# Half-batch 4 of a fused attention and gated feed-forward kernel: k and q transposed by DMA through a DRAM scratch instead of on TensorE

## The chip, the cores and the metric

The kernel runs on one core of a Trainium2 chip. The metric is the device time of one execution in microseconds (us), as the median of several executions. A profile of one execution, with the start and length of every instruction, is used to explain it. TensorE (PE in the profile, PEld for its weight loads) multiplies matrices, VectorE (DVE), ScalarE (ACT) and GpSimd (POOL) work on tiles, SyncE (SP) issues DMAs, and GpSimd issues DMAs too.

## The reference

For 8 batches, 8 heads, 576 positions and a head dimension of 64, the reference does causal attention with a decay, and then a gated feed-forward block on the 4,608 tokens:

```
scores = q @ k.T / sqrt(D)
bias   = -(cumsum(max(s, 0))[i] - cumsum(max(s, 0))[j])
scores = where(causal, -1e9, scores + min(bias, 0))
attn   = exp(scores - max); attn = attn / (sum(attn) + 1e-9)
x      = attn @ v                     # tokens by 512
out    = (silu(x @ w_gate) * (x @ w_val)) @ w_out
```

The inputs are float32, w_gate and w_val are 512 x 1536, w_out is 1536 x 512, the output is 4,608 x 512 float32.

## The kernel before

**Work and its units.** The 64 pairs of batch and head are numbered 0 to 63; I call each a head. Four heads are a half-batch, so there are sixteen, 0 to 15, two to a batch. A head's scores are made in four pieces (`score_piece`, L338), each a few matmuls of k by q into one PSUM bank (L359) and an exponential on ScalarE (L369). GpSimd clears the masked part of the first and the last piece (L374, L379). The product with v (`av_piece`, L396) goes into another bank, and `av_out` divides: a reciprocal (L412) and a multiply (L413) on VectorE, which free that bank. A head pair's result is transposed into XT, for batches 0 and 1 on TensorE (`x_pe`, L446, with a copy at L453), later by DMA (`x_out`, `x_in`).

**Feed-forward.** Nine blocks of 512 tokens (`ffn_items`). In each, twelve pairs of gate and value products (L630), with tanh on ScalarE (L651) and two VectorE operations (L653, L664), then the products with w_out (L687 in blocks 0 and 1, L736 later). Block 0 works on the first 512 tokens while the heads from 8 on are attended to.

**How k and q get their shape.** The score matmuls read the tiles KQ, with the head dimension on the partitions. There are two sets of KQ tiles, for even and odd half-batches; each set has two tiles, one for the first two heads and one for the last two. The loads bring k and q with positions on the partitions (`load_qk`, L140), so each half-batch is cast to bf16 (`cast_one`: L246 on GpSimd for half-batches 2 to 5, L244 on ScalarE from 6 on) and transposed, in one of two ways:

- On TensorE, for half-batches 0 to 4 (0 in halves, L301): `pe_transpose` (L287) writes five or four 128x128 transposes into a PSUM bank, and `pe_out` copies the upper and the lower half out, on ScalarE (L314) or VectorE (L316). For half-batch 4 the list `PREP_AT[3]` puts the four groups behind chosen score pieces of half-batch 3.
- By DMA, for half-batches 5 to 15: `scratch` (L260) stores the cast tiles to DRAM (ks and qs), `transposes` (L270) brings them back transposed into pk and pq, and `split` (L274) copies the two halves into KQ on VectorE. The splits stand in the list `later` and are taken from it by `do_later`.

Four further rows of each KQ tile come by small DMAs (`aug`, L183).

**What sets the order.** The order is written by hand: each engine takes its instructions in the order in which the Python code issues them. `attn_items` (L548) is a generator over the heads; `pump` runs it to a position that follows from how far the feed-forward block has come (L1016 to L1034). `side` issues, after given score pieces, the loads, scratch stores, DMA transposes and splits; `side_v` (L518) casts v. In the code h is the half-batch whose scores are being made and step the head within it. An engine's or a queue's instruction that waits holds back everything that stands behind it on the same engine.

**Around the change.** While half-batch 3 is attended to (heads 12 to 15), the SP queue holds the loads of k and q of half-batches 4 and 5, the five loads of V 2 (v of batch 2, `load_v`, after the last piece of head 12), the loads of half-batch 6, and then the scratch stores and transposes of half-batch 5. There is one buffer for loaded v (rawv), so V 2 waits for the casts of V 1. GpSimd casts V 2 (L168) while half-batch 4 is attended to. Eight PSUM banks are shared: `take` gives the one that has been free longest, and in the second part of block 0 four of them are held by the products with w_out.

Of the kernel before, what the change touches and what calls it, by code (L numbers as in the profile page):

```python
# [19 lines left out]
def kernel(  # L20
# [14 lines left out]
    B, H, S, D = q.shape  # L35
# [6 lines left out]
    NHB = BH // HB  # L42
    NR = HB // 2
# [33 lines left out]
        tc.tile_pool(name="dram", bufs=1, space=bass.MemoryType.DRAM)  # L77
    )

    NPE = 5  # L80
    XB = 2
    KS = {i: dram.tile([NR * S, 128], BF16, name=f"ks{i}") for i in range(NPE, NHB)}
    XS = {
        i: dram.tile([NCH * 128, 128], BF16, name=f"xs{i}") for i in range(XB * H // 2, BH // 2)
    }
    QS = {i: dram.tile([NR * S, 128], BF16, name=f"qs{i}") for i in range(NPE, NHB)}

# [16 lines left out]
    first = first_sbuf.enter_context(tc.tile_pool(name="first", bufs=1))  # L104
# [5 lines left out]
    with tc.manual_schedule():  # L110
# [36 lines left out]
        def load_qk(hb):  # L147
            load_one(hb, "k")
            load_one(hb, "q")

        def load_v(b, cs, eng=nc.sync):
            if 0 in cs:
                loaded["v", b] = raw.tile([128, NCH, H, D], FP32, tag="rawv", bufs=1, name="rawv")
            t = loaded["v", b]
            for c in cs:
                n = 128 if c < 4 else TAIL
                eng.dma_start(
                    t[0:n, c, :, :],
                    v[b, :, c * 128 : c * 128 + n, :].rearrange("h p d -> p h d"),
                )  # L160

        def cast_v(b, c, eng):
            n = 128 if c < 4 else TAIL
            dst, src_t = VT[b % 2][0:n, c, :, 0:D], loaded["v", b][0:n, c, :, :]
            if eng is nc.scalar:
                nc.scalar.copy(dst, src_t)
            else:
                eng.tensor_copy(dst, src_t)  # L168
# [89 lines left out]
        def scratch(hb):  # L258
            for name, SC in (("k", KS), ("q", QS)):
                nc.sync.dma_start(  # L260
                    SC[hb].rearrange("(x j) c -> x (j c)", j=J),
                    cts[name, hb].rearrange("x j r d -> x (j r d)"),
                )
# [3 lines left out]
        def transposes(hb):  # L267
            for name, SC in (("k", KS), ("q", QS)):
                prs[name, hb] = cp.tile([128, NR * S], BF16, tag="p" + name, bufs=1, name="p" + name)
                nc.sync.dma_start_transpose(prs[name, hb], SC[hb])  # L270
# [185 lines left out]
        later = []  # L456

        def do_later(n):
            while n > 0 and later:
                f, *args = later.pop(0)  # L460
                f(*args)
                n -= 1
# [5 lines left out]
        def side(h, step, ci):  # L468
            bh = HB * h + step
            for c in V1_AT.get((bh, ci), ()):  # L470
                cast_v(1, c, nc.gpsimd)
            if bh == H + 4 and ci == 3:
                load_v(2, range(5))
            if h == 4 and (step, ci) in ((0, 1), (2, 1)):
                load_qk(6 + step // 2)
            if h >= 5 and h + 3 < NHB and (step, ci) == (0, 1):
                load_qk(h + 3)
            hb = h + 1
            if NPE <= hb < NHB:
                late = hb == NPE  # L480
                if late and (step, ci) == (0, 1):
                    scratch(hb)
                if late and (step, ci) == (0, 3):
                    transposes(hb)
                if (step, ci) == (0, 1):
                    aug(hb, GP4)
                first = 1 if hb < NPE + 3 else 0
                if step in (first, first + 1) and ci == (3 if late else 1):
                    for r in range(NR):
                        later.append((split, hb, "kq"[step - first], r))  # L490
            hb = h + 2
            if hb == NPE and step == 3 and ci % 2 == 1:
                cast_one(hb, "kq"[ci // 2], nc.gpsimd)
            if NPE < hb < NHB:
                six = hb == NPE + 1
                if (step, ci) == ((2, 0) if six else (0, 2)):
                    cast_one(hb, "k", nc.scalar)
                if (step, ci) == ((2, 2) if six else (1, 2)):
                    cast_one(hb, "q", nc.scalar)
                if (step, ci) == ((3, 0) if six else (2, 0)):  # L500
                    scratch(hb)
                if (step, ci) == (3, 3 if six else 0):
                    do_later(NR * 2)
                    transposes(hb)
            if ci != 1:
                return
            bn = h // 2 + 1
            if 3 <= bn < B:
                if h % 2 == 0:
                    if step == 2:  # L510
                        load_v(bn, (0, 1))
                    if step == 3:
                        load_v(bn, (2, 3, 4))
# [13 lines left out]
        def prep_one(hb, i, eng=None):  # L527
# [7 lines left out]

        PREP_AT = {
            2: {(1, 2): 0, (2, 0): 2, (2, 2): 1, (3, 0): 3},
            3: {(1, 3): 0, (2, 1): 1, (2, 3): 2, (3, 1): 3},
        }

        AV_AT = {
# [6 lines left out]
        def attn_items():  # L548
            for kk in range(H, BH + 2):
                h, step = divmod(kk, HB)  # L550
                if kk < BH:
                    if step == 0:
                        do_later(NR * 2)
                    if step == 1 and 3 < h + 1 < NPE:
                        cast_one(h + 1, "k", nc.gpsimd)
                        cast_one(h + 1, "q", nc.gpsimd)
                    if step == 2 and 3 < h + 1 < NPE:
                        aug(h + 1, GP4)
                    for ci in range(4):
                        score_piece(kk, ci)  # L560
                        side(h, step, ci)
                        side_v(h, step, ci)
                        yield kk + 0.1 + ci / 8
                        if (step, ci) in PREP_AT.get(h, ()):
                            prep_one(
                                h + 1, PREP_AT[h][step, ci],
                                (nc.scalar, nc.vector)[ci // 2] if h == 2 else None,
                            )
                            yield kk + 0.1 + ci / 8
                for x in X_AT.get(kk, (kk - 2,)):  # L570
                    if x % 2 == 1 and H <= x < BH:
                        if x < XB * H:
                            x_pe(x // 2)
                            yield kk + 0.5
                        else:
                            x_in(x // 2)
                for p in AV_AT.get(kk, (kk - 1,)):
                    if H <= p < BH:
                        av_piece(p, (0, 1, 2))
                        yield kk + 0.6  # L580
                        av_piece(p, (3,))
                        yield kk + 0.7
                        av_piece(p, (4,))
                        av_out(p)
                        if p >= XB * H and p % 2 == 1:
                            x_out(p // 2)
                        yield kk + 0.8
# [416 lines left out]
        for tt in range(NTT):  # L1004
            lo = H * (tt + 1) + LAGS[tt]
            hi = min(H * (tt + 2) + LAGS[tt + 1], BH + 2)
            span = 36 if tt < FIRST7 else 34.5
            if hi == BH + 2:
                span = 30
            n0 = 5 if tt == 0 else 0  # L1010
            n = 0
            todo = {FIRST7 - 1: W_SUMS, FIRST7: W_DIFFS}.get(tt, [])
            if tt == FIRST7:
                for _ in range(3):
                    weight_op(*todo.pop(0))
            for i, cost in enumerate(ffn_items(tt)):  # L1016
                n += cost
                if todo and (i >= 24 if tt < FIRST7 else i % 2 == 1):
                    weight_op(*todo.pop(0))
                if tt == 0 and n > 30:  # L1020
                    pass
                elif i >= 2 * NFT or i % (2 if tt == 1 else 4) == 1:
                    do_later(1)
                if seconds:
                    seconds.pop(0)()
                for f in hook.pop(n, ()):
                    f()
                done = min(1.0, max(0, n - n0) / (span - n0))
                if tt == 0:
                    done = (  # L1030
                        0.57 * max(0, n - n0) / (24 - n0) if n < 24
                        else min(1.0, 0.57 + 0.43 * (n - 24) / (span - 24))
                    )
                pump(lo + (hi - lo) * done)  # L1034
# [31 lines left out]
```

## Time and profile before

| what | value |
|---|---|
| median of 3 runs | 376.51 us (376.23, 376.51, 377.41) |
| span of the profiled execution, first to last instruction | 375.9 us |
| median less span: what lies around the span | 0.6 us |
| TensorE busy | 364.4 us, 97% of the span, at a granted clock of 1.00 throughout |
| VectorE, ScalarE, GpSimd busy | 290.4, 240.3 and 212.1 us |
| DMA queue of SP, queue of GpSimd | 41.46 and 22.21 MB, 45.9% and 22.6% of the 16 DMA engines' time |
| HBM | 37.90 MB read, 19.86 MB written |

The profile gives the span of its one execution and no time of its own for what lies around it, so a sum is made against the span, and the rest is taken from the median. A span of 375.9 us in 40 slices makes a slice of 9.4 us; a digit of 9 in the rows by slice means busy for nine tenths of it or more. The chain is followed back from the last instruction; a piece of it names the engine, what it writes, and the line. Lines of the views are those of the kernel before.

### The profile page before, as it was taken

To read this page: it belongs to the slowest core of one execution; us is meant where nothing else is said; L and a number is where in the kernel's file an instruction comes from. 1 tells how busy PE (TensorE), PEld (TensorE's weight loads), DVE (VectorE), ACT (ScalarE), POOL (GpSimd) and SP (SyncE) were. 2 spreads that over 40 slices of the span, in tenths; PEclk is the share of its full clock that TensorE was granted. 3 is DMA by queue.
4 is the path that set the end of the run, shared out by engine and by line. 5 is a ranking of instruction groups with operands and counts; after the bars stand their busy time and mean duration, and the time that the engine had idled before them with its cause. 6 is when DMAs were issued, how large, how long until landed. Compare 5 with 4: busy or idle time off the path is not lost.

```text
span 375.9 us, 8800 instructions
## 1 busy us (share of the span) xinstructions
PE 364.4 (97%) x3300; PEld 231.1 (61%) x3300; DVE 290.4 (77%) x578; ACT 240.3 (64%) x471; POOL 212.1 (56%) x325
## 2 busy tenths in 40 slices
PE   7699999999999999999999999999999999999995
PEld 6475556655555556855685558655865585476464
DVE  8867867458995899679976997599858867975984
ACT  8687777597986887578757876687465523323321
POOL 8982556665365657494649555955675416315320
PEclk9999999999999999999999999999999999999999
DMA  7899999799599998796869665995132103002003
GB/s 237 197 267 265 201 248 272 216 312 242 169 185 267 246 255 221 168 275 217 224 145 262 192 162 163 264 188 145 39 104 77 35 19 127 2 0 90 24 0 113
DMA packets 97146, 64.23 MB, mean 171 GB/s; under 512 B 77232, under 2 KB 82736, under 8 KB 97104
## 3 DMA queue, kind: packets, MB, share of 16 engines
q1 hardware_dynamic: 84976, 41.46, 45.9%
q0 software_dynamic: 12128, 22.21, 22.6%
q8 instruction: 26, 0.43, 0.5%
q14 instruction: 16, 0.13, 0.1%
HBM read 37.90 MB, written 19.86 MB: 154 GB/s over the span
## 4 chain that ended last, share of the span: by engine, by line
PE 90%; POOL 3%; ACT 2%; DVE 2%; DMA 1%; issue 1%; DVEq 0%; POOLq 0%; ACTq 0%
PE bank L630 47%; PE bank L736 17%; PE bank L359 11%; PE bank L396 8%; PE bank L687 6%; ACT pt L369 2%; DMA kq<-HL 1%; DVE kq L316 1%; PE bank L446 1%; DVE pp L653 1%; PE bank L287 1%; POOL vt L168 1%; DVE ht L664 1%; PE bank L353 1%; ACT kq L314 0%
## 5 line engine op out<-in xcount | busy, mean ns | idle before, releaser
L369 ACT ACTIVATE pt<-bank 128x512 bf16<-128x512 f32 (+1 forms) x256 | 120.3, 510 | 32.1 <-PE bank L359 18.9
L630 PE MATMUL bank<-XT,wg 128*128 128x512 bf16 x432 | 111.4, 379 | 0.5 <-DVE pp L653 0.3
L630 PE MATMUL bank<-XT,wv 128*128 128x512 bf16 x432 | 110.9, 379 | 0.1
L651 ACT ACTIVATE th<-bank 128x512 bf16<-128x512 f32 x108 | 64.7, 599 | 55.7 <-PE bank L630 51.1
L653 DVE SCALAR_TENSOR_TENSOR pp<-th,bank 128x512 bf16<-128x512 bf16 x108 | 73.7, 682 | 18.7 <-ACT th L651 18.2
L664 DVE SCALAR_TENSOR_TENSOR ht<-pp,bank 128x512 bf16<-128x512 bf16 x108 | 74.1, 687 | 10.6 <-PE bank L630 0.4
L359 PE MATMUL bank<-kq 128*128 128x128 bf16 (+4 forms) x576 | 75.8, 240 | 2.7 <-DMA kq<-HL 2.3
L673 POOL TENSOR_TENSOR ht<-ht 128x512 bf16<-128x512 bf16 x35 | 40.4, 1155 | 52.3 <-DVE su L671 52.2
L359 PEld LDWEIGHTS <-kq 128*128 128x128 bf16 x576 | 45.8, 98 | 33.1 <-DMA kq<-HL 2.6
L630 PEld LDWEIGHTS <-wv 128*128 128x128 bf16 x432 | 38.4, 98 | 36.4 <-issue 0.6
L630 PEld LDWEIGHTS <-wg 128*128 128x128 bf16 x432 | 38.3, 98 | 34.2 <-issue 0.7
L374 POOL TENSOR_SCALAR_AFFINE_SELECT pt<-pt 128x512 bf16<-128x512 bf16 x56 | 37.0, 661 | 30.8 <-ACT pt L369 23.4
L396 PEld LDWEIGHTS <-pt 128*128 128x128 bf16 x960 | 41.7, 98 | 17.3
L396 PE MATMUL bank<-vt,pt 128*128 128x65 bf16 x960 | 46.9, 194 | 0.3 <-POOL vt L168 0.3
L430 POOL DMA_DIRECT2D xs<-ot x24 | 21.7, 904 | 30.0 <-DVE ot L413 27.7
L736 PEld LDWEIGHTS <-ht 128*128 128x128 bf16 x336 | 31.2, 98 | 4.3
L413 DVE TENSOR_TENSOR ot<-bank,rc 128x320 bf16<-128x320 f32 x64 | 31.5, 492 | 2.2
L183 POOL DMA_DIRECT2D kq<-HL x48 | 28.7, 599 | 0.0
L687 PE MATMUL bank<-wo,ht 128*128 128x512 bf16 x96 | 25.8, 379 | 0.0
L736 PEld LDWEIGHTS <-su 128*128 128x128 bf16 x252 | 23.6, 98 | 3.3
L412 DVE RECIPROCAL rc<-bank 128x5 f32<-128x5 f32 x64 | 12.1, 189 | 15.3 <-PE bank L396 14.8
L801 POOL TENSOR_TENSOR ysb<-ysb 128x512 f32<-128x512 f32 x12 | 15.2, 1271 | 15.3 <-DVE ysb L795 15.3
(93 smaller groups left out, 389.1 us busy)
## 6 DMA issues: line engine op xcount, KB each, us to landing
out_dram<-ysb POOLq DMA_DIRECT2D x32, 256.0 KB, 3.9
rawv<-in_v_dram SPq DMA_DIRECT2D x28, 256.0 KB
rawk<-in_k_dram SPq DMA_DIRECT2D x12, 576.0 KB
rawq<-in_q_dram SPq DMA_DIRECT2D x12, 576.0 KB
xs<-ot POOLq DMA_DIRECT2D x24, 160.0 KB, 4.0
ks<-ck SPq DMA_DIRECT2D x11, 288.0 KB
qs<-cq SPq DMA_DIRECT2D x11, 288.0 KB
rawk<-in_k_dram POOLq DMA_DIRECT2D x3, 576.0 KB, 6.8
```

The source lines that it names most:

```text
L359: nc.tensor.matmul(sc[:, o : o + w], T[:, 1, e * S + 128 * tj : e * S + 128 * (tj + 1)], T[:, 0, e * S + lo : e * S + hi], start=not maske ...
L369: nc.scalar.activation(pt[:, c0 : c0 + n], sc, AF.Exp, scale=0.125)
L374: nc.gpsimd.affine_select(pt[:, 1088:1600], pt[:, 1088:1600], pattern=[[0, 4], [1, 128]], compare_op=ALU.is_ge, fill=zreg, base=0, channel ...
L396: nc.tensor.matmul(av[:, bi * (D + 1) : (bi + 1) * (D + 1)], pt[:, c0 : c0 + 128], VT[b % 2][:, tj, h, :], start=(tj == 0), stop=(tj == bi),)
L413: nc.vector.tensor_mul(ot[:, :, e * D : (e + 1) * D], av3[:, :, 0:D], rc[:, :, None].to_broadcast([128, NCH, D]),)
L630: nc.tensor.matmul(view(bs, TT), w[:, c, f0 : f0 + 128], xt[:, c, :], start=(c == 0), stop=(c == 3),)
L651: nc.scalar.activation(th, pg, AF.Tanh, scale=0.5)
L653: nc.vector.scalar_tensor_tensor(pp, in0=th, scalar=1.0, in1=pg, op0=ALU.add, op1=ALU.mult)
L664: nc.vector.scalar_tensor_tensor(hp[:, 2 * k2 : 2 * k2 + 2, :].rearrange("p a n -> p (a n)"), in0=pp, scalar=0.5, in1=pv, op0=ALU.mult, op ...
L673: (nc.vector if ft == NFT - 1 else nc.gpsimd).tensor_sub(hp[:, 1:3, :], hp[:, 1:4:2, :], hp[:, 0:3:2, :])
L687: nc.tensor.matmul(view(pys[ts_], DM), hps[ft // 2][:, 2 * (ft % 2) + half, c0 : c0 + 128], WO[j][:, ft % WKO, :], start=(ft == 0), stop=( ...
L736: nc.tensor.matmul(ps, lhs(p), rhs(p), start=(first and p == 0), stop=(last and p == NP - 1), skip_group_check=True,)
```

## The change

Half-batch 4 goes over to the DMA path. The 18 transposes on TensorE and the eight copies out of PSUM go; two scratch stores and two DMA transposes are added on SP's queue, and four splits on VectorE. The scratch stores are issued after the last score piece of head 13, the transposes after the first score piece of head 14. The loads of V 2, so far issued after the last piece of head 12, now stand behind these transposes on the same queue. The four splits go into `later` after the last pieces of heads 14 and 15; the loop of block 0 now takes them from there one at a time, and the rest is taken before head 16. The casts, the small DMAs of `aug` and the treatment of half-batches 5 to 15 stay: where NPE (5) stood for the first half-batch of the DMA path, NSC (5) now stands for the first that is treated by the general rule.

```diff
-    NPE = 5
+    NPE = 4
+    NSC = 5
...
-            if bh == H + 4 and ci == 3:
-                load_v(2, range(5))
+            if h == 3:
+                if (step, ci) == (1, 3):
+                    scratch(4)
+                if (step, ci) == (2, 0):
+                    transposes(4)
+                    load_v(2, range(5))
+                if (step, ci) in ((2, 3), (3, 1)):
+                    for r in range(NR):
+                        later.append((split, 4, "kq"[step - 2], r))
...
-            if NPE <= hb < NHB:
-                late = hb == NPE
+            if NSC <= hb < NHB:
+                late = hb == NSC
...
         PREP_AT = {
             2: {(1, 2): 0, (2, 0): 2, (2, 2): 1, (3, 0): 3},
-            3: {(1, 3): 0, (2, 1): 1, (2, 3): 2, (3, 1): 3},
         }
...
-                    if step == 1 and 3 < h + 1 < NPE:
+                    if step == 1 and h == 3:
                         cast_one(h + 1, "k", nc.gpsimd)
                         cast_one(h + 1, "q", nc.gpsimd)
-                    if step == 2 and 3 < h + 1 < NPE:
+                    if step == 2 and h == 3:
                         aug(h + 1, GP4)
...
                 if tt == 0 and n > 30:
-                    pass
+                    if later and later[0][1] == 4:
+                        do_later(1)
```

The DRAM tiles ks and qs of half-batch 4 are added by the first lines, since their range starts at NPE. In what is left out, NPE is replaced by NSC in the conditions for half-batches 5 and later, with the same value as before.

More of the change, by code (lines that the diff above doesn't have):

```diff
@@ L486, in side @@
                     aug(hb, GP4)
-                first = 1 if hb < NPE + 3 else 0
+                first = 1 if hb < NSC + 3 else 0
                 if step in (first, first + 1) and ci == (3 if late else 1):
@@ L491, in side @@
             hb = h + 2
-            if hb == NPE and step == 3 and ci % 2 == 1:
+            if hb == NSC and step == 3 and ci % 2 == 1:
                 cast_one(hb, "kq"[ci // 2], nc.gpsimd)
-            if NPE < hb < NHB:
-                six = hb == NPE + 1
+            if NSC < hb < NHB:
+                six = hb == NSC + 1
                 if (step, ci) == ((2, 0) if six else (0, 2)):
```

## The prediction

> **What bounds the kernel now.** I read the page first: busy shares, the slices, the chain by engine.
>
> ```profile
> span 375.9 us, 8800 instructions
> PE 364.4 (97%) x3300; PEld 231.1 (61%) x3300; DVE 290.4 (77%) x578; ACT 240.3 (64%) x471; POOL 212.1 (56%) x325
> DMA  7899999799599998796869665995132103002003
> PE 90%; POOL 3%; ACT 2%; DVE 2%; DMA 1%; issue 1%; DVEq 0%; POOLq 0%; ACTq 0%
> ```
>
> TensorE works 97% of the span and is 90% of the chain that ended last, so a TensorE instruction taken out anywhere is worth its own time, as long as nothing else becomes late. The DMA row says where that can fail: one slice is 9.4 us, and from the third to the fifteenth (19 to 141 us) the DMA engines are full but for a 7 in the eighth (66 to 75) and a 5 in the eleventh (94 to 103). The change takes time from the first resource and gives it to the second, at about 60 us.
>
> Next the chain around the four groups of transposes that go (start, length, what):
>
> ```profile
> 58.62 0.25 PE bank L359 x3
> 58.87 0.28 PE bank L287 x5
> 59.15 0.35 PE bank L446 x5
> ...
> 62.91 0.28 PE bank L287 x5
> 63.19 0.22 PE bank L359 x2
> ...
> 64.08 0.22 PE bank L287 x4
> 64.30 0.35 PE bank L446 x5
> ...
> 68.06 0.22 PE bank L287 x4
> 68.28 0.22 PE bank L359 x2
> ```
>
> From 54.98 to 87.23 us every piece of this chain is TensorE's, end to end, with no wait between. The L287 pieces are the transposes of half-batch 4: 18 in four pieces.
>
> Then SP's queue, for what is moved (start, length of the issue):
>
> ```profile
> 55.31 8.55 SPq L157 DMA_DIRECT2D rawv<-in_v_dram  x5
> 63.97 0.56 SPq L140 DMA_DIRECT2D rawk<-in_k_dram  x1
> ...
> 69.70 0.36 SPq L260 DMA_DIRECT2D ks<-ck  x1
> 70.98 0.35 SPq L260 DMA_DIRECT2D qs<-cq  x1
> 71.82 1.31 SPq L270 DMA_TRANSPOSE pk<-ks  x1
> ```
>
> These are V 2, k of half-batch 6, and the scratch path of half-batch 5. The semaphore records of the trace give the landings: k and q of 5 at 59.95 and 61.55, V 2's five loads from 62.45 to 66.91, k and q of 6 at 68.29 and 69.71, ks and qs of 5 at 71.80 and 73.09, pk and pq of 5 at 76.53 and 77.81. SP's loads land in the order of issue: one queue.
>
> **Step 1, TensorE.** The four pieces are 0.28 + 0.28 + 0.22 + 0.22 = 1.00 us. The instruction order of the changed build differs on TensorE by these 18 transposes alone. Gain 1.00.
>
> [...]
>
> **Step 2, the copies.** ScalarE loses four (pairs of 1.52 and 1.46, 2.98 us), VectorE four (1.66 + 1.46 = 3.12), and gets four splits of L274 (0.44 to 0.95 each, some 2.2 together). Neither engine is in the chain here: worth nothing by themselves. But a split waits for a DMA at a place in VectorE's order where the PSUM copy waited for TensorE.
>
> **Step 3, half-batch 4 through DMA.** GpSimd's casts of k and q end at 57.41 and 59.67, so SP issues ks at 57.4 and qs at 59.7, behind q of 5, which lands at 61.55. Half-batch 6 shows the same queueing: behind a V load that landed at 86.17, its ks and qs landed at 86.97 and 87.89 (0.80, then 0.92). So ks 62.35, qs 63.3. In the half-batches without V loads between (5, 7, 9, 11, 13, 15), pk landed 2.2 (7) to 3.65 us (13) after qs, in the middle 3.15, and pq 4.05 (9) to 6.2 (7), middle 4.5. So pk of 4 lands at 65.5 to 66.95, I take 66.45, and pq at 67.35 to 69.5, I take 67.8.
>
> Who needs it: in VectorE's new order the first split stands ahead of the reciprocal and multiply (L412, L413) that free the bank of head 15's third score piece, and the second split ahead of those for the fourth. These pieces start at 68.28 and 69.14 now, at 67.28 and 68.14 without the transposes. Split, reciprocal and multiply took 1.13 together at 83.31, so the fourth piece needs pk by 68.14 - 2.3 = 65.85. **Stall S1** = 66.45 - 65.85 = 0.6 (0 to 1.1). pq is needed by 69.28, 0.46 before head 16's scores at 69.74: 0 at 67.8, 0.2 at 69.5.
>
> **Step 4, what is moved back.** V 2 now stands behind pq. It landed 5.36 after q of 5: 67.8 + 5.36 = 73.2, its first load near 68.7. GpSimd casts it from 76.06, then 75.06: covered by 6 us. k and q of 6 took another 2.8: 74.6 and 76.0; ScalarE casts them at 78.38 and 81.61, then 77.4 and 80.6: covered, 2.8 on k, and behind that cast stand the exponentials. ks and qs of 5, held behind them on SP: another 1.72, and an output store (256 KB, issued at 74.81; 0.75 by the 348 GB/s around it): qs at 78.4, against 73.09 now. pk of 5 lands 3.15 later (2.2 to 3.65): 81.6. Needed:
>
> ```profile
> 81.45 0.45 DVE L274 COPY kq<-pk 64x1152 bf16<-64x1152 bf16 x1
> ...
> 86.26 0.95 DVE L274 COPY kq<-pq 64x1152 bf16<-64x1152 bf16 x1
> ```
>
> That is 80.45 with the full gain. VectorE has work without a gap from 80.05 to 91, and TensorE already waits for its split of q (0.13 at 87.23, the chain's one "issue" piece there), so lateness goes on in full. **Stall S2** = 81.6 - 80.45 = 1.15. Its ends: with pq at 67.35, V 2 at the 1,076 rows of 256 B that the packet records show in the microsecond from 84 (4,608 rows, 4.3 us), no store and pk 2.2 after qs, pk lands at 78.4, S2 = 0. With pq at 69.5, V 2 at the pace of V 3's last three loads (2,560 rows in 3.97, so 7.1), the store and 3.65, it lands at 85.5, S2 = 5.1. I stay with 1.15: V 2's own row is nearest. S1 and S2 don't add: a stall moves the later needs too, so the larger counts. Then the DMA engines recover: 94 to 96 us shows a share of 0.31, and pk of 6 has 2.3 us (landed 93.30, split 95.64).
>
> A row on the transposes' pace: 590 KB of them took 4.5 us, 130 GB/s, while k and q of 6 (1,180 KB) took 2.8, 421 GB/s. [...]
>
> **Sum.** -1.00 + 1.15 = +0.15. The profiled span is 375.86; the median of the three runs is 376.51, 0.65 above, which I take to lie around the span in both kernels. Span 376.0, time 376.65, rounded to **376.6**.
>
> **Rivals.**
> 1. *The transfers are hidden, the full gain stays.* For it: V 2, k 6 and pk of 4 have ends that give no stall, and DMA share is only 0.4 from 68 to 72 now, room for part of the added work. Against it: that room is under 3 us, and ks, qs, pk and pq add 1.7 + 4.5. 376.51 - 1.0 = 375.5; with the 0.13 at 87.23 gone as well, 375.4.
> 2. *The DMA queue becomes the bound, slower.* One mechanism: pk of 5 comes late to its split at 81.45 since V 2 and two loads stand between the two pairs of transposes. It decides from a landing of 80.45 and costs over 0.3% from 82.6. With the pair of 4 at half-batch 7's pace (+1.7) S2 is 2.85; with V 2 at V 3's pace as well (+1.75), 4.6. Between, 3.1: +2.1, 378.6. For it: the DMA row, and SP's in-order queue. Against: it takes the slow row twice.
> 3. *The change doesn't reach the path:* if TensorE's room were filled by another wait at 54 to 90 us, the 1.00 is lost and nothing else happens: 376.5. The chain without gaps speaks against it; it looks like my forecast.
>
> **Numbers.** 0.3%, or 1.13 us, is about what a measurement of this kernel can tell from no change. Forecast with rival 3 (375.8 to 377.5): 0.45, all but 0.06 of it within 0.3%, the rest slower. Rival 1: 0.22, half of it past -0.3%, since 1.0 to 1.13 is the whole gain. Rival 2: 0.33, slower. So faster 0.11, within 0.50, slower 0.39. The range reaches over rival 1 down to 375.3 and over most of rival 2 up to 378.8, leaving out the far end of its slow rows.
>
> **What would show it.** TensorE: no L287 after 49 us, the chain near 67 us 1.0 earlier. S1: a gap before head 15's last score pieces, released by VectorE, its L274 behind a DMA. S2: the first L274 of half-batch 5 waiting for pk, and TensorE's gap near 87 grown from 0.13. Wrong if pk of 4 lands later than 67, if ScalarE waits for k of 6 or GpSimd for V 2, or if the chain is TensorE's without a gap from 55 to 95.

## The result, and the profile after

The changed kernel takes 378.44 us (median of 20 executions, 376.17 to 383.41) against 376.52 us of the kernel before in the same comparison (20 executions, 375.77 to 378.23): ratio 1.005, 95% interval 1.0031 to 1.007. That is 1.9 us more, and the whole interval is above 0.3%. The forecast was 376.6, within 0.3%; the time that came is next to that of my rival 2, 378.6, to which I gave 0.33 (0.39 for slower in all). The range, 375.3 to 378.8, holds the median, by the end that was drawn over rival 2.

The profiled execution took 376.73 us with a span of 374.9, so it is one of the fastest of its kernel, and its span is shorter than that of before (375.9). The span alone says nothing here; the stages do. First the page of after: busy shares, the DMA engines by slice, the chain by engine.

```profile
span 374.9 us, 8724 instructions
PE 361.5 (96%) x3241; PEld 230.3 (61%) x3282; DVE 289.3 (77%) x578; ACT 237.5 (63%) x467; POOL 212.6 (57%) x325
DMA  7899998999989996797769674996132103002003
PE 83%; DMA 6%; SPq 5%; POOL 2%; ACT 1%; issue 1%; DVE 1%; DVEq 0%; POOLq 0%
```

TensorE's share of the chain fell from 90% to 83%, and DMA and SP's queue, 1% together before, have 11%. That is no measure of the loss (the transposes were 1.00 us, 0.3% of the span): from the first splits of half-batch 4 the chain now leads back through the DMA queue to the loads before them. Next the busy time by stretch (in each row: the stretch, its length, TensorE's busy time and instructions, then its weight loads, VectorE, ScalarE, GpSimd, the granted clock, the DMA share, GB/s):

```profile
58.00:67.00 9.00, 8.30 (x97) 5.21 (x98) 4.15 (x10) 3.55 (x7) 5.80 (x11) 1.00 0.77 207
67.00:76.00 9.00, 7.82 (x78) 4.69 (x78) 4.28 (x10) 5.12 (x12) 6.42 (x13) 1.00 1.18 300
```

Before had TensorE busy for 9.00 of 9.00 in both stretches. The DMA share shows the moved work: 1.02 and 0.82 before, 0.77 and 1.18 now. The chain of after through this place (start, length, what) no longer consists of TensorE:

```profile
55.57 5.81 DMA ks<-ck
...
61.44 3.43 DMA pk<-ks
...
64.90 0.45 DVE kq L275
...
65.52 0.49 issue
66.01 1.37 DVE kq L275
...
67.41 0.21 DVE rc L413
...
67.64 0.51 DVE ot L414
...
68.18 0.19 PE bank L360
```

L275, L360, L413 and L414 are L274, L359, L412 and L413 of before. The scratch store and the transpose of half-batch 4 lead to its first two splits on VectorE; behind these stand the reciprocal and the multiply that free the bank of head 15's last score piece. (By the diff the splits of k go into the list `later` after head 14's last piece, those of q after head 15's second piece, not after its last.) This is stall S1 at the place that was predicted. The waits of after between 60 and 100 us (total, times, longest) name it:

```profile
PE bank L360 <- DVE ot L414: 1.7, 2, 1.1
```

From 68.18 to 90 us the chain has no piece of another engine, and the gap at the place of S2, 0.13 before, is 0.13 still (at 86.43). In this execution S2 cost nothing beside S1.

**How the runs are compared.** The early part of the kernel, whose instructions are the same in all kernels here, varies: the first exponential of head 12 started between 49.57 and 53.62 us in the profiled executions. So I count from there. "12 to 16" is the time from the first exponential of head 12 to that of head 16 (S1 falls in it), "12 to 24" the same to head 24. From head 24 to the end all profiled executions need 269.9 to 270.4 us, but for late_late5 (271.3), defer (271.8) and late (270.7). All in us:

| kernel | median (executions) | ratio to before, interval | head 12 starts | pk of 5 lands, after that | 12 to 16 | 12 to 24 |
|---|---|---|---|---|---|---|
| before | 376.52 (20) | | 51.49 | 25.04 | 19.56 | 54.15 |
| after | 378.44 (20) | 1.005, 1.0031 to 1.007 | 49.65 | 30.89 | 20.60 | 55.18 |
| again | 378.16 (12) | 1.0051, 1.0032 to 1.0071 | 51.61 | 30.14 | 19.50 | 54.36 |
| no_dma | 375.91 (12) | 0.9989, 0.9971 to 1.0007 | 49.57 | 24.78 | 18.56 | 53.14 |
| dma_only | 377.85 (12) | 1.0048, 1.0026 to 1.007 | 51.67 | 32.92 | 19.55 | 57.14 |
| late | 380.03 (6) | 1.0099, 1.0072 to 1.0126 | 51.77 | 33.49 | 18.56 | 58.06 |
| defer | 380.07 (10) | 1.0082, 1.0049 to 1.0115 | 50.98 | 30.07 | 19.50 | 54.76 |
| late5 | 378.06 (12) | 1.0024, 0.9998 to 1.005 | 50.74 | 30.59 | 19.51 | 54.19 |
| three | 379.13 (12) | 1.0053, 1.0024 to 1.0082 | 50.84 | 30.71 | 18.57 | 54.74 |
| ctl | 376.65 (12) | 0.9996, 0.9974 to 1.0018 | 50.19 | 25.50 | 19.56 | 54.17 |
| late_late5 | 379.35 (6) | 1.0064, 1.0042 to 1.0087 | 50.04 | 30.67 | 18.56 | 54.85 |
| late_swap | 378.71 (12) | 1.0044, 1.0017 to 1.007 | 50.03 | 29.13 | 18.56 | 53.56 |
| k_only | 378.60 (6) | 1.0056, 1.0034 to 1.0078 | 50.03 | 28.67 | 20.64 | 55.22 |
| no_v2 | 377.60 (12) | 1.0024, 1.0001 to 1.0048 | 53.62 | 25.18 | 18.57 | 53.15 |

The ratios are each against executions of before on the same chip (medians 376.52 to 376.90).

### The profile page after: what moved, and what is told of

Same layout as the page of the kernel before. It is cut to its first block, busy times and chain, and to the rows that moved or that the text cites. A ratio compares the mean times of both kernels' runs of the same rounds, so it can differ in the third digit from the quotient of the medians.

```text
span 374.9 us, 8724 instructions
## 1 busy us (share of the span) xinstructions
PE 361.5 (96%) x3241; PEld 230.3 (61%) x3282; DVE 289.3 (77%) x578; ACT 237.5 (63%) x467; POOL 212.6 (57%) x325
## 4 chain that ended last, share of the span: by engine, by line
PE 83%; DMA 6%; SPq 5%; POOL 2%; ACT 1%; issue 1%; DVE 1%; DVEq 0%; POOLq 0%
PE bank L637 44%; PE bank L743 17%; PE bank L360 10%; PE bank L397 7%; SPq L158 5%; PE bank L694 4%; DMA rawk<-in_k_dram 3%; DMA ks<-ck 2%; ACT pt L370 1%; DMA pk<-ks 1%; DMA kq<-HL 1%; PE bank L354 1%; DVE kq L275 0%; POOL kq L215 0%; POOL ck L247 0%
## 5 line engine op out<-in xcount | busy, mean ns | idle before, releaser
L637 PE MATMUL bank<-XT,wv 128*128 128x512 bf16 x411 | 109.3, 379 | 1.1
L360 PE MATMUL bank<-kq 128*128 128x128 bf16 (+4 forms) x576 | 75.6, 240 | 3.1 <-DVE ot L414 1.7
L360 PEld LDWEIGHTS <-kq 128*128 128x128 bf16 x576 | 45.8, 98 | 32.3 <-issue 2.8
L414 DVE TENSOR_TENSOR ot<-bank,rc 128x320 bf16<-128x320 f32 x64 | 31.5, 492 | 2.2
L694 PE MATMUL bank<-wo,ht 128*128 128x512 bf16 x90 | 24.8, 379 | 0.3
L380 POOL TENSOR_SCALAR_AFFINE_SELECT pt<-pt 128x64 bf16<-128x64 bf16 x56 | 14.8, 264 | 16.6 <-ACT pt L370 16.4
```

The lines of the kernel that those rows point to most:

```text
L360: nc.tensor.matmul(sc[:, o : o + w], T[:, 1, e * S + 128 * tj : e * S + 128 * (tj + 1)], T[:, 0, e * S + lo : e * S + hi], start=not maske ...
L414: nc.vector.tensor_mul(ot[:, :, e * D : (e + 1) * D], av3[:, :, 0:D], rc[:, :, None].to_broadcast([128, NCH, D]),)
L637: nc.tensor.matmul(view(bs, TT), w[:, c, f0 : f0 + 128], xt[:, c, :], start=(c == 0), stop=(c == 3),)
L694: nc.tensor.matmul(view(pys[ts_], DM), hps[ft // 2][:, 2 * (ft % 2) + half, c0 : c0 + 128], WO[j][:, ft % WKO, :], start=(ft == 0), stop=( ...
```

## The experiments

**again**: the changed kernel unchanged, for a second trace.

> The changed kernel itself, for a second profile and a second time beside the others. The first profile shows TensorE waiting 0.59 and 1.13 us before head 15's third and fourth score pieces for the multiply that stands behind the first split of half-batch 4. Theory A (the split's place in VectorE's order): these two waits are there again, longer in a longer execution. Theory B (the queue that was moved back: V 2, k and q of 6, half-batch 5's transposes come late): waits after 75 us, at casts or at half-batch 5's first split. Both: 1.5 to 2.5 us slower than before, single executions spread from the time before to 6 us above it.

The landings of this trace are close to those that were worked out: pk of 4 at 66.39 (66.45 predicted), pq of 4 67.64 (67.8), V 2 73.53 (73.2), k of 6 74.85 (74.6), q of 6 76.65 (76.0), qs of 5 78.17 (78.4), pk of 5 81.75 (81.6). The second stall is in its chain:

```profile
77.45 4.30 DMA pk<-ks
...
81.78 0.45 DVE kq L275
82.23 0.60 DVE pp L660
```

The transposing DMA of half-batch 5 leads to its split, and the split to the feed-forward's multiply behind it on VectorE. Two traces of one kernel thus show S1 and S2 in different sizes, 12 to 24 being 55.18 and 54.36. In again that is 0.21 over before, close to the sum of the prediction (+0.15); its median is 1.5 over before (378.16 against 376.61), and this trace doesn't show where the rest is lost.

**no_dma**: the gain alone. No scratch and no transposes for half-batch 4, V 2 at its old place; the splits of 4 copy half-batch 3's k and q, so heads 16 to 19 work with wrong k and q.

```diff
+            src_t = prs[name, hb] if hb > 4 else KQ[1][r][:, kq, 0 : NR * S]
...
-                if (step, ci) == (1, 3):
-                    scratch(4)
-                if (step, ci) == (2, 0):
-                    transposes(4)
+                if (step, ci) == (0, 3):
                     load_v(2, range(5))
```

> The changed kernel without the scratch stores and transposes of half-batch 4, V 2 loaded where it was before; the four splits copy k and q of half-batch 3 in their place, so heads 16 to 19 compute with the wrong k and q. It shows the gain of the 18 TensorE transposes alone. Theories A and B: 1.0 us faster than before (0.8 to 1.2). If it is not faster, the step that priced the transposes is wrong.

12 to 24 is 53.14 against 54.15: the gain is 1.01 us, as the four L287 pieces said (1.00), and TensorE waits for nothing between 60 and 100 us. The median is 0.7 lower (375.91 against 376.61), with an interval that reaches to no change.

**dma_only**: the cost alone. The kernel before, with the scratch stores and transposes of half-batch 4 added in front of V 2, and their result not used.

```diff
-            if bh == H + 4 and ci == 3:
-                load_v(2, range(5))
+            if h == 3:
+                if (step, ci) == (1, 3):
+                    scratch(4)
+                if (step, ci) == (2, 0):
+                    transposes(4)
+                    load_v(2, range(5))
```

> The kernel before with the scratch stores and DMA transposes of half-batch 4 added on SP in front of V 2, and their result not used; TensorE still transposes. It shows the cost of the moved queue alone. Theory A: no change (within 0.3 us). Theory B: 1.5 to 3 us slower than before, with waits for half-batch 5's pk, for k of 6 or for V 2.

It is slower by 1.2 us in the median, a little under the 1.5 to 3 of Theory B, with no split, copy or transpose of TensorE changed: the DMA queue alone does it. Its profiled execution (380.56 us) is the second longest of its twelve, and shows the stall large (chain, start and length; lines as in before):

```profile
72.25 6.99 DMA ks<-ck
...
79.26 5.33 DMA pk<-ks
...
84.62 0.45 DVE kq L274
85.07 0.60 DVE pp L657
```

The split of half-batch 5 would have started 29.96 after head 12, as in before; pk landed 2.96 later than that, and 12 to 24 grew by 2.99. S2 is shown, and so is that it goes on in full where S1 doesn't stand before it.

**late**: against S1. The four splits of half-batch 4 are issued directly behind head 15's last score piece, not through the list.

```diff
-                if (step, ci) in ((2, 3), (3, 1)):
+                if (step, ci) == (3, 3):
                     for r in range(NR):
-                        later.append((split, 4, "kq"[step - 2], r))
+                        split(4, "k", r)
+                        split(4, "q", r)
```

> The changed kernel with the four splits of half-batch 4 issued after head 15's last score piece, behind the reciprocals and multiplies that free the banks; the DMAs are as in the changed kernel. Theory A: the waits before head 15's last pieces go, the transposes have until 69.3 us, the full gain shows: 1.0 us faster than before (0.5 to 1.2) and a spread like that of before. Theory B: as slow as the changed kernel, 1.5 to 2.5 us above before.

S1 is gone: 12 to 16 is 18.56, the same as in no_dma. That S1 were the whole loss fell at once, since the kernel is 3.4 us over before, more than either theory said. In this execution, the longest of its six (382.27), pk of 5 landed 33.49 after head 12, 4.54 late, and TensorE waited for VectorE (timeline; the bracket is the idle time before the group and its releaser):

```profile
86.38 1.02 PE L638 MATMUL bank<-XT,wv 128*128 128x512 bf16 x3 [2.67 <-DVE pp L661]
...
87.79 1.91 PE L638 MATMUL bank<-XT,wg 128*128 128x512 bf16 x4
```

Four such matmuls take 1.03 elsewhere. The row by stretch says why they took 1.91 (the third figure from the end is the granted clock):

```profile
87.50:91.00 3.50, 3.50 (x18) 1.65 (x17) 3.40 (x9) 1.80 (x4) 1.11 (x2) 0.51 1.14 311
```

After this wait of 2.67 the granted clock was 0.5 for 3.41 us; half of that, up to 1.7 us, is my estimate of what was lost on top of the wait. Waits of 2.9 and this make 4.6 of the 4.92 by which 12 to 24 is longer than in no_dma.

**defer**: are block 0's output stores, which GpSimd issues from 74 us on, what delays pk of 5? After, with the four stores issued in block 1, near 93 us.

> The changed kernel with block 0's four output stores (256 KB each, GpSimd's queue) issued in block 1 near 93 us instead of 74 to 81. In the profiles so far their packets run between the loads of q of 6 and the transposes of half-batch 5. Theory B1 (pk of 5 is late at its split since SP's queue was moved back and the stores come between): pk of 5 lands 2 to 3.5 us sooner, near 79.5, no wait of VectorE for it; what is left is the wait before head 15's last pieces: 0 to 0.7 us slower than before. Theory B2 (the stores are hidden anyway, the SP queue alone does it): as the changed kernel, 1.5 to 2 us slower.

pk of 5 lands 30.07 after head 12, against 30.14 and 30.89 with the stores where they were: the 2 to 3.5 us that Theory B1 expected from moving them aren't there. Moved, they do harm here: block 2 waits for XT (waits from 100 to 125 us), and head 24 to the end takes 271.76.

```profile
PE bank L637 <- DMA XT<-xs: 1.5, 1, 1.5
```

**late5**: against S2. After, with the splits of half-batch 5 moved behind head 19's second piece (the first of k and of q there, the others through the list).

```diff
-                if step in (first, first + 1) and ci == (3 if late else 1):
+                if late:
+                    if (step, ci) == (3, 1):
+                        split(hb, "k", 0)
+                        split(hb, "q", 0)
+                        later.append((split, hb, "k", 1))
+                        later.append((split, hb, "q", 1))
+                elif step in (first, first + 1) and ci == 1:
```

> The changed kernel with the splits of half-batch 5 later in VectorE's order: those of the first two heads after head 19's second score piece, near 85 instead of 81.4 us, the others after them; no DMA is moved. If the cost sits where VectorE's order meets pk of 5 (theory B1 and B2 both), a landing up to 85 is covered: 0 to 0.7 us slower than before, with the waits before head 15's last pieces still there. If the late queue costs in other places (V 2's casts, k of 6, half-batch 6), it stays 1.5 us or more slower.

No wait for pk of 5 is left, and 12 to 24 is 54.19, so S1's 0.95 is what still stands. In the median 1.2 us are left (378.06 against 376.90 of before), between the two cases that were expected, with an interval that touches no change.

**three** (late, late5 and defer together) and **ctl** (the edits of late5 and defer on the kernel before, without the change).

> The changed kernel with all three edits: half-batch 4's splits after head 15's last piece, half-batch 5's splits later, block 0's stores later. If the two waits at the splits and the stores are all of the cost, the full gain of the 18 transposes shows: 1.0 us faster than before (0.6 to 1.3), from head 12 to head 22 as in the kernel without the DMAs (44.5 us, against 45.5 before). If the DMA queue costs elsewhere too: as before or slower.

> The kernel before with the later splits of half-batch 5 and the later stores, without the change. Control for the run with all three edits: as before within 0.3 us. If it is 0.7 us or more faster, that run owes its gain to these edits and not to the change.

ctl is before, to 0.02 us from head 12 to 24: these edits cost nothing where the queue is on time. In three S1 is gone and S2 nearly, yet head 22 to 24 takes 9.91 instead of 8.6: pk of half-batch 6 landed at 96.86, and its splits now came late. The lateness moved on to the next half-batch.

**late_late5**: late and late5 without defer.

> After, with both sets of splits moved in VectorE's order and nothing else: the four of half-batch 4 behind head 15's last score piece, those of half-batch 5 behind head 19's (the first two) and later. Theory (the DMA queue's lateness is paid where a split stands in VectorE's order ahead of work that TensorE needs): S1 goes (head 12 to head 16 in 18.6 us, as without the scratch path), S2 goes (head 16 to head 22 in 26.0), and what is left is half-batch 6, 2.5 us later than before at its split: 0.3 to 1.0 of wait. Median 0.0 to 1.0 under before (ratio 0.9973 to 1.000). Rival (the splits' place matters less than the traffic itself, which slows all): at or above before, ratio 1.003 or more, as after.

Neither S1 nor S2 in the profile, but head 22 to 24 again takes 10.05, with this wait between 55 and 130 us:

```profile
PE bank L360 <- DVE pp L667: 0.7, 1, 0.7
```

Another 1.2 us is lost between 240 and 260 us. The gain that I expected did not come: 2.6 us over before.

**late_swap**: late, and on SP's queue the scratch stores of half-batch 5 ahead of the loads of half-batch 6 instead of behind them.

```diff
+            if h == 4 and (step, ci) == (0, 1):
+                scratch(5)
             if h == 4 and (step, ci) in ((0, 1), (2, 1)):
                 load_qk(6 + step // 2)
...
-                if late and (step, ci) == (0, 1):
-                    scratch(hb)
```

> After, with the splits of half-batch 4 behind head 15's last score piece, and on SP's queue the two scratch stores of half-batch 5 ahead of the loads of half-batch 6 instead of behind them: the same bytes, another order. Theory (in-order queue): ks of 5 lands right behind V 2, at 74.3, qs at 75.2, pk of 5 some 3.15 later but behind the two loads (2.8), so 78.0 to 80.0 against a need of 80.5: no wait at L275 of half-batch 5, head 16 to head 22 in 26.0 us, ratio 0.9975 to 1.001. Rival (the queue's total decides, not its order): pk of 5 at 81 to 85 as in after and in the kernel with late splits alone, ratio 1.004 to 1.010.

In the profile the theory's numbers are nearly met: ks of 5 lands 0.7 behind V 2 at 72.47, pk of 5 29.13 after head 12, 0.18 late, TensorE waits 0.3 for its split, and 12 to 24 is 53.56, 0.6 under before. The chain shows how little room is left (start, length, what):

```profile
72.34 0.20 DVE ot L414
72.54 6.62 DMA pk<-ks
...
79.19 0.45 DVE kq L275
```

This execution took 375.60 us, the fastest of its twelve. The median is 378.71, so the other executions lose some 3 us that this trace does not show. In the median the rival's number came, not mine.

**k_only**: k alone of half-batch 4 by DMA, q's two groups on TensorE again.

```diff
-            for name, SC in (("k", KS), ("q", QS)):
+            for name, SC in (("k", KS), ("q", QS))[: 1 if hb == 4 else 2]:
...
+            3: {(2, 1): 1, (3, 1): 3},
```

> After, with k alone of half-batch 4 through the scratch; q's two groups of transposes stay on TensorE. Half of the gain (0.28 + 0.22 = 0.50) and half of the added traffic (one scratch store, one transpose: about 3 us less in front of V 2). Theory: pk of 4 lands at 64 to 65 (S1 near 0), pk of 5 at 78 to 79.7 (S2 0): 0.5 under before, ratio 0.9987. Rival (any transposing DMA in front of V 2 costs its stall, whatever its size): ratio 1.002 to 1.005.

Half right. pk of 5 came in time (28.67 after head 12). But pk of 4 landed 14.89 after head 12, hardly earlier than with q's store in the queue (15.22 and 14.78). In absolute time it met the 64 to 65 that was expected (64.92), but head 12 had started early (50.03), and S1 stayed (timeline):

```profile
66.05 0.88 DVE L275 COPY kq<-pk 64x1152 bf16<-64x1152 bf16 x1
66.97 0.19 DVE L413 RECIPROCAL rc<-bank 128x5 f32<-128x5 f32 x1
67.20 0.49 DVE L414 TENSOR_TENSOR ot<-bank,rc 128x320 bf16<-128x320 f32 x1
67.60 1.45 DVE L317 COPY kq<-bank 64x512 bf16<-64x512 bf16 x2
```

TensorE waited 1.3 for the multiply at 67.20, which stands behind the second split as in after; the copies of q out of PSUM come only behind it. 12 to 16 is 20.64, as long as in after, with half of the gain.

**no_v2**: after without the five loads of V 2; batch 2's product is made with batch 1's v.

```diff
-                    load_v(2, range(5))
+                    loaded["v", 2] = loaded["v", 1]
```

> After, without the five loads of V 2: the cast for batch 2 reads the tile that still holds v of batch 1, so batch 2's product is made with batch 1's v. It takes 5.4 us out of SP's queue behind the transposes of half-batch 4. Theory: pk of 5 lands at 76 to 77, no wait, S2 gone; S1 stays at 0.6 (the splits of 4 are where they were): 0.4 under before, ratio 0.9975 to 1.000. Rival (the added splits or the removed copies on VectorE and ScalarE cost by themselves): ratio 1.003 or more, with no wait for pk of 5.

With 5.4 us out of the queue pk of 5 lands 25.18 after head 12, as in before, and 12 to 24 is 53.15: the full gain, neither S1 nor S2. S1 went too, which I had not expected: head 12 started late here (53.62) for a reason of its own, and pk of 4 landed only 14.02 after it. In the median 0.9 us over before remains, against the 0.4 under it that was expected.

## Why the prediction found both stalls and fell short in its sum

**Step 1 held.** 1.00 predicted, 1.01 measured (no_dma).

**Step 2 held**: no wait of ScalarE or GpSimd for the moved loads appears, and the copies that went brought nothing beyond the 1.01.

**Step 3, S1: the place was right, the size was not.** I took a split of 0.45 and a stall of 0.6 (0 to 1.1). "12 to 16" is 2.04 longer than in no_dma in after, 0.94 in again. In after, pk of 4 landed 15.22 after head 12; by the step's own need (65.85 less 51.49) it was 14.36. That gives 0.86, and the second split took 1.37 instead of 0.45, 0.92 more: 1.78 of the 2.04. The split had started while GpSimd ran its cast of half-batch 5, and the prediction had no term for that (the last section has the rows).

**Step 4, S2: the landing was right for again, the need was not.** pk of 5 was predicted 30.11 after head 12 (81.6 less 51.49) and came 30.14 after it in again. That this fits to 0.03 is luck: in the eight executions whose queue has the order of after it came 30.07 to 30.89 after head 12 in six, but 32.92 in dma_only and 33.49 in late, at starts of head 12 (51.67, 51.77) like that of again (51.61). The need goes with TensorE, the landing with the queue. Where head 12 started at 49.65, 50.04, 50.74, 50.84, 50.98 and 51.61 us, pk of 5 landed at 80.54, 80.71, 81.33, 81.55, 81.05 and 81.75: over 2 us of starts the landing moved by 1.2. The profile of before, from which I took the need, was an execution with a late start, 51.49. In after the landing alone gives S2 = 30.89 - 28.95 = 1.94 instead of 1.15 (28.95 is the start of the split after head 12 without lateness, from no_dma).

The row on the transposes' pace held more than the pace: its 4.5 us run from the landing of qs to that of pq. For half-batch 5 of before these are 4.72 apart (73.09 and 77.81). The 2,304 packets of 256 B in between, the pair's 590 KB, ran from 73.14 to 76.82: 3.68 us, 160 GB/s; the landing of pq was recorded 0.99 after the last of them. pq of 5 landed 1.28 us after pk (77.81 - 76.53), which is 230 GB/s for its 295 KB.

**"The larger counts" held.** From head 12 to 24, after lost 2.04 against no_dma, with S1 = 2.04 and S2 = 1.94. again lost 1.22, with S1 = 0.94 and S2 = 1.19. No sum would fit either. But in after the larger one was S1, which the prediction had at 0.6 and so left out of its sum.

**What lies around the span was wrong.** I took 0.65, the median of before less the span of its profile. Time less span is 1.8 in after (376.73 - 374.9), and near that in most of the executions that give both. The profile of before was thus an execution of about 377.6, slower than its median: the same late start.

**The sum** should have been -1.00 + 2.04 = +1.04 by the trace of after; by that of again, -1.00 + 1.22, it was nearly right. The medians say +1.9 and +1.5, and here lies what I had no term for. The mean granted clock of an execution shows whether TensorE fell to half speed for a time: one stretch of 3.41 us at 0.5 makes it 0.9955 by estimate (1 - 1.7 / 376), and late and no_v2, whose profiles hold one such stretch each, have 0.996 and 0.995. Below 0.9965 were 5 of 20 executions of after (median 380.82) and 2 of 85 of before. The other 15 of after have a median of 377.66, 1.1 above before. In late and no_v2 the half clock came with waits of 2.67 and 3.42 us (the last section has the rows); that waits brought it in the five executions of after too is an assumption of mine. It can't be all: three of those 15 took 380.40 to 381.74, and of again's twelve only one was below 0.9965, while the other eleven have a median of 377.99, 1.4 above before, where their trace has 0.21.

**The rivals.** Rival 2 was right in that the DMA queue costs more than the transposes gave: dma_only shows it without the rest of the change, no_dma shows the change without it, and in the profile of no_v2 both stalls are gone with V 2 out of the queue (its median is still 0.9 over before). Its one mechanism, pk of 5 late at its split by 2.85 to 4.6, isn't what the traces of after and again show: there pk of 5 landed at 80.54 and 81.75, ahead of the 82.6 from which it was to cost 0.3%, and S1 is 2.04 of the 2.04 that were lost there and 0.94 of the 1.22. So 378.4 next to 378.6 is in part luck. A lateness of rival 2's size is what the longer executions of dma_only (2.99) and late (4.54) show. The point from which I said it decides (a landing at 80.45) was an absolute time; it should have been one relative to TensorE. Rival 1 fell with the landings. Rival 3 fell with no_dma.

**What stays open.** Several kernels lose more in the median than their profile shows from head 12 to 24: late_swap 2.6 us (2.0 over before, where the profile is 0.6 under), no_v2 1.9, three 1.6, again 1.3, late5 1.1, after 0.9. The profiled executions of three, late_late5, late_swap and k_only are the fastest of their kernels, so their longer ones were not seen. Whether these lose at the same splits, in the early part or by the half clock wasn't tried. Two long executions were profiled: dma_only's (380.56) and late's (382.27) lost at the split of half-batch 5, pk landing some 3 us later than in again at the same start; no_v2's, 1.0 above its median (378.64), lost early, in a wait of 3.42 at 10 us and the half clock behind it. It also stays open why pk of 5 is that late in some executions, and why ks of 5 lands 0.7 behind q of 6 in after and again, but 2.1 to 2.5 behind it in late, late_late5 and three. No complete version beat before; the best with the change in it, late5, is 1.2 us behind it.

## What to carry to other kernels

Before work is moved from a full engine to a full queue, take the slack of the first consumer behind the moved place, in time relative to the bound engine: pk of 5 had 4.9 us (25.04 against 29.96), of which the gain itself takes 1.0, and the change put 5.1 to 5.9 on its landing. Do the same for the moved work's own consumer: in after it was pk of 4, at its two splits, that cost most. Curing one late consumer moved the lateness to the next one: in late TensorE waited 2.67 us for the feed-forward's multiply behind the split of half-batch 5, and in three and late_late5 head 22 to 24 took 9.91 and 10.05 us instead of 8.6. The DMA share was still 0.99, 1.14 and 0.92 in the three stretches of after from 76 to 103 us. Only work taken out of the queue (no_v2), or out of the order in front of the consumer (late_swap), gave the gain or most of it back, and both in their profile alone: their medians stay 0.9 and 2.0 us over before. And a need read from one profile is worth no more than that execution's start: see how far the stage before it varies.

## What the runs showed of the hardware

**The clock.** TensorE stood still for 2.67 us up to 86.38 in late, and from 87.56 on the granted clock was 0.5 for 3.41 us. In no_v2 it stood still for 3.42 us from 9.97, and the clock was 0.5 from 13.22, for 3.41 us again. Gaps of 2.27 (before, at 10.4 us), 2.01 and 1.81 us (dma_only) were followed by no drop. So the drop came once with a gap of 2.67 and once with one of 3.42, and at 2.27 and below it did not come; what sets it these runs don't show. The gap near 10 us (0.8 us of it a wait for the small DMAs of the first half-batches in after, 2.3 in before, 3.4 in no_v2) is also a part of why head 12 started so differently; in again it was 1.4, and head 12 as late as in before.

**A copy on VectorE beside GpSimd.** The same 64x1152 split took 0.44 us at 68.05 in after, but 1.37 at 66.01 and 1.03 at 69.33; GpSimd's casts of half-batch 5 (1.15 each) had started at 65.9 and 68.9. Of the splits in these traces, 13 began while such a cast had 0.3 us or more to run; they took 0.64 to 1.40, and each ended 0.31 to 0.32 us after the cast's end. Three began just ahead of a cast (by 0.005 to 0.025 us, in no_v2, late and late_late5); they kept 0.44 to 0.46, and the cast took 1.43 to 1.44. In these 16 cases the one that started second was the one that took longer, so a split cost 0.44 to 1.40 us, by what GpSimd was doing at that moment.
